# Two sets of PE transposes or one, for the flags of an expert selection inside an attention kernel

## The chip, the cores and the metric

The kernel runs on one core of a Trainium2 chip. A core has five engines that run their own instruction lists side by side and meet at semaphores: TensorE (PE; in the profile its weight loads have a row of their own, PEld), VectorE (DVE), ScalarE (ACT), GpSimd (POOL) and SyncE (SP, which here only issues transfers). The metric is the device time of one execution, in microseconds; less is better.

## The reference

Attention over 8 batches of 12 heads (448 positions, head size 64), causal, and behind it a mixture of experts with a limit on the tokens of an expert. The attention's output, 3584 rows of 768, is its input.

```python
def _moe_ref(x, w_gate, w1, w2, capacity):
    logits = x @ w_gate                              # 3584 x 8
    expert_idx = np.argmax(logits, axis=1)
    ...
    gate_w = probs[np.arange(N), expert_idx]
    for e in range(E):
        tok_idx = np.where(expert_idx == e)[0]
        if len(tok_idx) > capacity:                  # capacity is 80
            gw = gate_w[tok_idx]
            keep = np.argpartition(-gw, capacity)[:capacity]
            tok_idx = tok_idx[keep]
        h = np.maximum(x[tok_idx] @ w1[e], 0.0)
        out[tok_idx] = gate_w[tok_idx, None] * (h @ w2[e])
```

So each expert keeps the 80 tokens of the largest gate weight. What the change touches is how that choice is worked out while attention is still running.

## The kernel before

**Attention.** Two heads make a pair, six pairs a batch. The instruction order of every engine is written out by hand (`manual_schedule`): the loop over pairs runs over eight slots (k = 0 to 7) for each pair, and a slot issues one tile of the scores of this pair (`sp`, lines 423 to 436), in slots 0, 2, 4 and 6 a group of four transposes of the pair before (`tp`, line 465), in slot 7 the products with the values of the pair before that (`xp`, line 495). Behind each piece follows what reads it: DVE takes the scores with the mask and a maximum (`ns`, line 445; `nb` is its accumulator), ACT takes the exponential (`prob`, line 448) and copies the transposed tile out of PSUM (`PT`, line 477; for some pairs DVE does one of the four). The scores have three PSUM banks in turn, `tp` two. Every 16 slots a new third of the queries and keys is cast to fp16 and to the remainder: `L387` on DVE, `L384`, `L390`, `L391` and `L395` on POOL.

**The selection.** While the scores of batch b + 1 run, the selection of batch b is worked out in small steps, each with a due slot counted from the end of the batch: `STEPS` (lines 33, 34: `EARLY` takes its place for b = 6, the batch before the last). One slot can hold several steps; they are issued in the order of the dictionary, behind the slot's own work. For b = 7, the last batch, the steps run behind all the attention, in the order of `TAIL`.

The steps around the change, with their slots in STEPS:

- `weight`, `weighted` (28, 31): the gate weight of each token, and `ow`, the one-hot of its expert times that weight; POOL (DVE for some).
- `columns` (30, line 698): the flags. POOL writes the one-hot three times side by side into `oh3` (line 702), and one-hot times the number of the token in two pieces into `mv` (lines 703, 705).
- `parts` (33, lines 710 to 716): `ow` in three bf16 pieces, also into `mv`, four POOL instructions.
- `r0t`, `r0c` (32, 33): four PE transposes of `oh3` (128 x 128, line 731) into one PSUM bank `selt`, and DVE's copy of 24 rows of it into `ex[:, 0]` (line 734).
- `r1t`, `r1c` (34, 35): the same of the `ow` pieces in `mv`, into `ex[:, 1]`.
- `rl`, `lt`, `cp`, `ro` (36 to 41): the tokens against the table of the best 80 so far (`rl` reads `ex[:, 0]`), counted; `c3w` to `c0l` (38 to 46): the tokens of the batch against one another (`rn`, line 745, reads both halves of `ex`; `less`, line 748, is DVE's comparison).
- `gt`, `own`, `rank`, `places`, `rr`, `tn`, `tab`, `rp`, `row` (47 to 81): the new table. `tn` (77, line 862) reads `mv`; 81 is slot 33 of the next batch, so `rp` and `row` of batch b - 1 lie beside `r0t` and `r0c` of batch b.

All these PSUM tiles share the two banks "misc" of the pool `ps_m` in turn: each waits until the tile two before it has been read. `mv` and `oh3` have one buffer each, padded with zeros, since a transpose always reads 128 columns.

Of the kernel before, what the change touches and what calls it, by code (L numbers as in the profile page):

```python
# [10 lines left out]
BF16 = mybir.dt.bfloat16  # L11
# [6 lines left out]
P = 128  # L18
# [11 lines left out]
ROWGAP = 1  # L30
ROWS0 = [2, 3, 7, 13]
ROWS1 = [59, 62, 64, 65]
STEPS = {'gp': 18, 'gs': 18, 'lp': 21, 'lg': 22, 'logit': 23, 'shifted': 25, 'chosen': 26, 'sums': 27, 'one_hot': 28, 'weight': 28, 'weighted': 31, 'columns': 30, 'parts': 33, 'r0t': 32, 'r0c': 33, 'r1t': 34, 'r1c': 35, 'rl': 36, 'lt': 36, 'c3w': 38, 'c3l': 39, 'cp': 40, 'ro': 41, 'c2w': 41, 'c2l': 43, 'c1w': 43, 'c1l': 44, 'c0w': 46, 'c0l': 46, 'gt': 47, 'earlier': 51, 'own': 47, 'rank': 51, 'places': 63, 'places_more': 66, 'rr': 73, 'tn': 77, 'tab': 78, 'rp': 80, 'row': 81, 'rr_more': 75}
EARLY = {'gp': 18, 'gs': 18, 'lp': 21, 'lg': 21, 'logit': 22, 'shifted': 24, 'chosen': 26, 'sums': 27, 'one_hot': 28, 'weight': 29, 'weighted': 31, 'columns': 30, 'parts': 32, 'r0t': 33, 'r0c': 33, 'r1t': 34, 'r1c': 34, 'rl': 35, 'lt': 35, 'c3w': 36, 'c3l': 37, 'cp': 38, 'ro': 39, 'c2w': 39, 'c2l': 40, 'c1w': 40, 'c1l': 41, 'c0w': 41, 'c0l': 42, 'places': 43, 'places_more': 43, 'gt': 44, 'earlier': 44, 'own': 44, 'rank': 46, 'rr': 46, 'tn': 48, 'tab': 50, 'rp': 51, 'row': 52, 'rr_more': 46}
ROWS_EARLY = [22, 26, 29, 43]
THIRD = [0, 0, 2, 2, 4, 6, 8]
THIRD_NEXT = [0, 0, 6, 2, 6, 4, 8]
# [15 lines left out]
def attention_then_moe(  # L53
# [19 lines left out]
    NT = (S + P - 1) // P  # L73
# [24 lines left out]
    def bank(shape, dtype, name):  # L98
        return (ps_x or ps_m).tile(shape, dtype, name=name, tag="x" if ps_x else "misc")
# [20 lines left out]
    NV = 5  # L120
# [11 lines left out]
    for r in range(2):  # L132
        t = akeep.tile([P, OFF_L + NT * P], F32, name=f"prob{r}")
# [7 lines left out]
    for r in range(2):  # L141
        t = akeep.tile([P, NT, PH * P], F32, name=f"vt{r}")
# [79 lines left out]
    lg = keep.tile([P, NT, H * E], F32, name="lg")  # L222
# [28 lines left out]
    def late_constants():  # L251


        def padded(shape, name):
            t = spool.tile(shape, BF16, name=name, tag=name, bufs=1)
            nc.gpsimd.memset(t, 0.0)
            return t

        def orders():
            nonlocal identb, before  # L260
            identb = const.tile([P, P], BF16, name="identb")
            nc.gpsimd.tensor_copy(identb, ident)

            before = const.tile([P, NT * P], BF16, name="before")
            nc.gpsimd.memset(before, 1.0)
            own = before[:, (NT - 1) * P:NT * P]
            nc.gpsimd.affine_select(own, own, [[-1, P]], ALU.is_gt, 0.0, base=0, channel_multiplier=1)

        def gate_weights():
            nonlocal wgd  # L270

            wgd = const.tile([P, NP, 4 * E], F32, name="wgd")
            nc.gpsimd.memset(wgd, 0.0)
            for i in range(2):
                for j in range(2):
                    nc.gpsimd.tensor_copy(wgd[j * DH:(j + 1) * DH, i:NP:2, 2 * i + j:4 * E:4],
                                          wg_sb[j * DH:(j + 1) * DH, i:NP:2, :])

        def slots():
            nonlocal mv_flat, mv, slots_e, slots_t  # L280
            many = max(1, NSL)
            slots_e = const.tile([SL, many, E, SL], COUNT, name="slots_e")
            slots_t = const.tile([P, many, NT, SL], COUNT, name="slots_t")
            for t, k in ((slots_e, E), (slots_t, NT)):
                nc.gpsimd.iota(t, [[SL, many], [0, k], [1, SL]], base=0, channel_multiplier=0,
                               allow_small_or_imprecise_dtypes=True)
            mv_flat = padded([P, (NT - 1) * NV * E + 2 * E + P], "mv")
            mv = mv_flat[:, 0:NT * NV * E].rearrange("k (t v e) -> k t v e", v=NV, e=E)

        def operands():  # L290
            nonlocal oh_flat, one_hots, expert_cols, tables, table_rows
            oh_flat = padded([P, (NT - 1) * 3 * E + P], "oh3")
# [398 lines left out]
    def select_groups(bt):  # L691

        b = bt.b
        last = b == B - 1
# [2 lines left out]

        def columns():
            oh = bt.oh
            m, oh3 = bt.m, bt.oh3 = mv, one_hots  # L700
            bc = [P, NT, E]
            eng.tensor_copy(oh3, oh.unsqueeze(2).to_broadcast([P, NT, 3, E]))
            nc.gpsimd.tensor_tensor(out=m[:, :, 0, :], in0=oh, in1=tbase[:, b, :].unsqueeze(2).to_broadcast(bc),
                                    op=ALU.mult)
            nc.gpsimd.tensor_tensor(out=m[:, :, 1, :], in0=oh, in1=pnum.unsqueeze(2).to_broadcast(bc), op=ALU.mult)
            bt.parts = sm("parts", [P, NT])
            bt.less = [sm(f"less{t}", [P, (t + 1) * P], BF16) for t in range(NT)]
            bt.ex = expert_cols
# [14 lines left out]
        def expert_rows(i):  # L723
            got = []

            def turn():
                selt = bank([P, NT * P], BF16, "selt")
                got.append(selt)
                for t in range(NT):
                    src = mv_flat[:, (t * NV + 2) * E:][:, 0:P] if i else oh_flat[:, t * 3 * E:][:, 0:P]  # L730
                    nc.tensor.transpose(selt[:, t * P:(t + 1) * P], src, identb)

            def copy():
                (nc.scalar.copy if last else nc.vector.tensor_copy)(bt.ex[0:3 * E, i], got[0][0:3 * E])
            return [turn, copy]


        def compare(t):
            w = (t + 1) * P
            got = []  # L740

            def weights():
                rn = bank([P, NT * P], F32, "rn")
                got.append(rn)
                nc.tensor.matmul(rn[:, 0:w], bt.ex[:, 0, t * P:w], bt.ex[:, 1, 0:w], start=True, stop=True)

            def less():
                nc.vector.scalar_tensor_tensor(
                    out=bt.less[t], in0=got[0][:, 0:w], scalar=bt.gw[:, t:t + 1],
                    in1=before[:, NT * P - w:NT * P], op0=ALU.is_lt, op1=ALU.mult, accum_out=bt.parts[:, t:t + 1])  # L750
            return [weights, less]
# [90 lines left out]
        def move(s):  # L842
# [43 lines left out]
            if not last and NSL == 1:  # L886
# [3 lines left out]

        run = lambda fs: lambda: [f() for f in fs]
        bt.lower, bt.moves = [], []
        r0, r1 = expert_rows(0), expert_rows(1)
        cmp = [compare(t) for t in reversed(range(NT))]
        tabs = [table_chunk(s) for s in range(NSL)] if b else []
        moves = [f for s in range(NSL) for f in move(s)]
        steps = {"columns": columns, "parts": parts, "r0t": r0[0], "r0c": r0[1], "r1t": r1[0], "r1c": r1[1],
                 "places": places, "places_more": places_more, "earlier": earlier, "own": own, "rank": rank}
        steps.update({"hold": hold, **{f"gt{t}": lambda t=t: later_part(t) for t in range(NT)}} if last else {"gt": later})
        for t in range(NT):  # L900
# [38 lines left out]
    for b in range(B):  # L939
        bt = Batch()  # L940
# [17 lines left out]
    def batch_plan(bt):  # L958
# [23 lines left out]
    with tc.manual_schedule():  # L982
# [126 lines left out]
        for i, x in enumerate(ROW_ENGINES):  # L1109
            g, t = divmod(i, NT)  # L1110
# [331 lines left out]
```

## Time and profile before

| what | us |
|---|---|
| time, median of 3 runs (lowest to highest) | 466.85 (466.36 to 467.3) |
| the profiled execution's own time | 466.07 |
| its span, first to last instruction | 464.2 |
| transposes of `oh3`, 8 batches of 4 | x32, 217 to 230 ns each |
| transposes of `mv`, 8 batches of 4 | x32, 216 to 219 ns each |
| DVE's copies of `selt`, b = 0 to 6 | x14, 401 to 409 ns each |

The page gives each engine's busy time as a share of the span, and the chain that ended last: followed back from the last instruction, at each step to what released it. A row of the timeline is start, duration, engine, line, operation, output and inputs, count; in brackets, how long the engine was idle before it and who ended that. A matmul's duration has its latency in it; the distance to the next start shows how long it holds PE. In the windows view a row is the stretch, its length, the engine's busy time in it with the number of instructions, PE's granted clock, and the share and the rate of the DMA engines.

### The profile page before, as it was taken

What the parts mean: (1) busy time and instruction counts of PE and PEld (TensorE: products, weight loads), DVE (VectorE), ACT (ScalarE), POOL (GpSimd) and SP (SyncE); (2) the same over time, 40 slices, a digit from 0 to 9 for tenths busy, and PEclk for the clock granted to TensorE, in tenths of its full rate; (3) what the DMA queues carried; (4) which work ended last, traced back from release to release, by engine and by line L of the source; (5) the groups of instructions that cost most, each with busy time, mean ns of one, the idle gap of its engine ahead of it and who ended that gap; (6) DMA issues with size and microseconds to landing.
All of it is one profiled execution on the core that took longest, in us unless ns stands there. A gap on an engine that the chain in (4) does not pass through costs nothing.

```text
span 464.2 us, 14187 instructions
## 1 busy us (share of the span) xinstructions
PE 441.8 (95%) x4981; PEld 346.8 (75%) x4981; DVE 413.1 (89%) x1285; ACT 392.4 (85%) x1077; POOL 310.3 (67%) x382
## 2 busy tenths in 40 slices
PE   4899999999999999999999999999989999999994
PEld 2566667866777786677777767777648999999994
DVE  6888899988998999899899989989579999999892
ACT  6898989878988997898889789888586989988792
POOL 7999999988987987898798789860145133410011
PEclk9999999999999999999999999999999999999999
DMA  7758899989769578966957997539937999999941
GB/s 221 185 153 238 249 262 299 280 248 306 202 207 305 161 232 259 265 182 213 297 165 225 264 260 200 178 129 373 413 130 254 399 390 395 394 422 423 424 163 44
DMA packets 42998, 120.84 MB, mean 260 GB/s; under 512 B 6146, under 2 KB 23810, under 8 KB 39472
## 3 DMA queue, kind: packets, MB, share of 16 engines
q1 hardware_dynamic: 41712, 116.21, 76.9%
q0 software_dynamic: 1056, 3.51, 2.4%
q8 instruction: 39, 0.64, 0.6%
q14 instruction: 31, 0.25, 0.2%
q10 hardware_dynamic: 160, 0.23, 0.2%
HBM read 96.36 MB, written 23.99 MB: 259 GB/s over the span
## 4 chain that ended last, share of the span: by engine, by line
PE 83%; DVE 6%; DMA 3%; ACT 3%; issue 2%; SPq 1%; POOLq 0%; DVEq 0%
PE xp L495 16%; PE tp L465 15%; PE sp L423 6%; PE sp L424 5%; PE rt L592 4%; PE op L1245 4%; PE op L1237 4%; PE hp L1237 3%; PE gp L545 3%; PE hp L1252 3%; PE hp L1251 3%; PE hp L1249 3%; PE sp L433 3%; DMA qk<-k_t 3%; DVE ns L445 2%
## 5 line engine op out<-in xcount | busy, mean ns | idle before, releaser
L448 ACT ACTIVATE prob<-ns,nb 128x128 f32<-128x128 f32 (+3 forms) x336 | 177.0, 529 | 22.6 <-DVE nb L445 20.1
L445 DVE CUSTOM_DVE_ANT_0 ns<-sp,mask 128x384 f32<-128x384 f32 (+2 forms) x288 | 116.0, 413 | 18.7 <-PE sp L424 14.7
L465 PE MATMUL tp<-ident,prob 128*128 128x128 f32 x768 | 118.1, 276 | 0.9 <-ACT prob L448 0.9
L477 ACT COPY PT<-tp 128x512 f32<-128x512 f32 x182 | 104.0, 572 | 17.5 <-PE sp L423 8.4
L395 POOL TENSOR_TENSOR qk<-qk,qk 128x448 f16<-128x448 f32 x92 | 97.3, 1080 | 13.1 <-DVE qk L387 7.4
L465 PEld LDWEIGHTS tp<-ident,prob 128*128 128x128 f32 x768 | 89.6, 142 | 11.4 <-ACT prob L448 1.9
L1165 DVE SCALAR_TENSOR_TENSOR wl<-wraw,wh 128x768 f16<-128x768 f32 (+1 forms) x91 | 92.0, 1067 | 2.5 <-ACT wh L1180 2.3
L495 PE MATMUL xp<-PT,vt 128*64 128x448 f32 (+3 forms) x768 | 91.2, 380 | 0.0
L495 PEld LDWEIGHTS xp<-PT,vt 128*64 128x64 f32 x768 | 53.8, 137 | 42.7 <-issue 22.6
L423 PE MATMUL sp<-qk 128*128 128x384 f16 (+2 forms) x288 | 75.8, 279 | 8.0 <-DVE qk L349 5.1
L1180 ACT ACTIVATE wh<-wraw 128x768 f16<-128x768 f32 (+1 forms) x91 | 78.9, 931 | 4.2 <-PE hp L1252 1.8
L424 PE MATMUL sp<-qk 128*128 128x384 f16 (+2 forms) x288 | 78.1, 277 | 1.6 <-DVE qk L349 0.8
L448 ACT ACTIVATION_READ_ACCUMULATOR prob<-ns,nb 128x1 f32 x336 | 63.9, 190 | 0.0
L1338 POOL DMA_INDIRECT out<-yo,idx x8 | 14.6, 1828 | 69.0 <-ACT yo L1335 65.1
L390 POOL TENSOR_TENSOR qk<-qk,qk 64x448 f16<-64x448 f32 x46 | 54.2, 1179 | 3.4
L391 POOL TENSOR_TENSOR qk<-qk,qk 64x448 f16<-64x448 f32 x46 | 51.0, 1108 | 3.2
L387 DVE CAST qk<-qk 128x896 f16<-128x896 f32 x46 | 41.2, 897 | 1.1 <-DMA qk<-k_t 1.1
L423 PEld LDWEIGHTS <-qk 128*128 128x128 f16 x288 | 28.5, 99 | 17.1 <-issue 8.6
L384 POOL CAST qk<-qk 64x896 f16<-64x896 f32 x40 | 37.4, 936 | 4.3 <-PE sp L436 3.1
L1249 PEld LDWEIGHTS <-wh 128*128 128x128 f16 x362 | 36.5, 101 | 0.0
L1251 PEld LDWEIGHTS <-wh 128*128 128x128 f16 x362 | 36.2, 100 | 0.0
L1252 PEld LDWEIGHTS <-wl 128*128 128x128 f16 x362 | 36.2, 100 | 0.0
(192 smaller groups left out, 926.8 us busy)
## 6 DMA issues: line engine op xcount, KB each, us to landing
wraw<-w SPq DMA_DIRECT2D x27, 1536.0 KB, 20.4
qk<-k_t SPq DMA_DIRECT2D x92, 224.0 KB, 5.9
out<-mask_l SPq DMA_DIRECT2D x56, 192.0 KB, 4.4
qk<-q_t SPq DMA_DIRECT2D x23, 448.0 KB, 4.4
vt<-v_t SPq DMA_DIRECT2D x24, 384.0 KB, 5.9
xs<-xr SPq DMA_DIRECT2D x42, 192.0 KB, 3.9
wraw<-w SPq DMA_DIRECT2D x24, 256.0 KB, 6.1
vt<-v_t SPq DMA_DIRECT2D x24, 64.0 KB, 5.5
```

Of the source, the lines that this page charges most:

```text
L390: nc.gpsimd.tensor_tensor(out=qa[hi, i], in0=qf[lo, i], in1=qa[lo, i], op=ALU.subtract)
L391: nc.gpsimd.tensor_tensor(out=qb[lo, i], in0=qf[hi, i], in1=qb[hi, i], op=ALU.subtract)
L395: nc.gpsimd.tensor_tensor(out=k_lo[j][:, i], in0=kf[j][:, i], in1=k_hi[j][:, i], op=ALU.subtract)
L423: nc.tensor.matmul(sp[:, 0:w], qx[:, p, t * P:w], kx[:, p, 0:w], start=True, stop=False)
L424: nc.tensor.matmul(sp[:, 0:w], qx[:, p, t * P:w], lx[:, p, 0:w], start=False, stop=True)
L445: pr.masked = nc.vector.tensor_tensor_reduce(out=ns[:, 0:w], in0=sp[:, 0:w], in1=m, scale=-1.0 / 8.0, scalar=HUGE, op0=ALU.add, op1=ALU.mi ...
L448: nc.scalar.activation(pr.P[:, off:off + w], ns[:, 0:w], AF.Exp, bias=nb, scale=-1.0, accum_out=total)
L465: nc.tensor.transpose(pr.tp[:, i], pr.P[:, off:off + P], ident)
L477: copy(dst, src)
L495: state["pe"] = nc.tensor.matmul(xp[rows, 0:w], st["vt"][:, c, p * P + j * DH:p * P + (j + 1) * DH], pr.PT[:, j, n0:n0 + w], start=(c == 0 ...
L1165: return nc.vector.scalar_tensor_tensor(out=l, in0=src, scalar=SW, in1=h, op0=ALU.mult, op1=ALU.subtract)
L1180: nc.scalar.activation(h, src, AF.Copy, scale=SW)
```

## The change

In b = 0 to 6 one set of four transposes does for both kinds of flags. `mv` becomes 128 columns for each of the four token tiles (16 groups of 8 experts): the five pieces stand in groups 2 to 6, the three copies of the one-hot in groups 8 to 10 of the same block, and `columns` writes them there. A transpose of the whole block then holds the `ow` pieces in rows 32 to 55 and the one-hots in rows 64 to 87. The set is called `r1t` and stands where `r0t` was (slot 32; in `EARLY` slot 33, with `parts` left at 32); `parts` goes from slot 33 to 31. The two copies `r0c` and `r1c` keep their slots and read the same bank, the first from row 64, the second from row 32. The memset of `mv` grows from 264 to 544 columns. The last batch keeps `oh_flat` and its two sets.

```diff
-STEPS = {... 'columns': 30, 'parts': 33, 'r0t': 32, 'r0c': 33, 'r1t': 34, 'r1c': 35, 'rl': 36, 'lt': 36, ...}
-EARLY = {... 'parts': 32, 'r0t': 33, 'r0c': 33, 'r1t': 34, 'r1c': 34, 'rl': 35, 'lt': 35, ...}
+STEPS = {... 'columns': 30, 'parts': 31, 'r1t': 32, 'r0c': 33, 'rl': 36, 'lt': 36, 'r1c': 35, ...}
+EARLY = {... 'parts': 32, 'r1t': 33, 'r0c': 33, 'r1c': 34, 'rl': 35, 'lt': 35, ...}
...
-            mv_flat = padded([P, (NT - 1) * NV * E + 2 * E + P], "mv")
-            mv = mv_flat[:, 0:NT * NV * E].rearrange("k (t v e) -> k t v e", v=NV, e=E)
+            mv_flat = padded([P, NT * P + 4 * E], "mv")
+            mv = mv_flat[:, 0:NT * P].rearrange("k (t v e) -> k t v e", t=NT, e=E)
...
-            m, oh3 = bt.m, bt.oh3 = mv, one_hots
+            m = bt.m = mv[:, :, 2:2 + NV, :]
+            oh3 = bt.oh3 = one_hots if last else mv[:, :, 8:11, :]
...
-                    src = mv_flat[:, (t * NV + 2) * E:][:, 0:P] if i else oh_flat[:, t * 3 * E:][:, 0:P]
+                    src = mv_flat[:, t * P + 4 * E:][:, 0:P] if i else oh_flat[:, t * 3 * E:][:, 0:P]
...
-                (nc.scalar.copy if last else nc.vector.tensor_copy)(bt.ex[0:3 * E, i], got[0][0:3 * E])
+                nc.scalar.copy(bt.ex[0:3 * E, i], got[0][0:3 * E])
+
+        def both_rows():
+            got = []
+
+            def turn():
+                selt = bank([P, NT * P], BF16, "selt")
+                got.append(selt)
+                for t in range(NT):
+                    nc.tensor.transpose(selt[:, t * P:(t + 1) * P], mv_flat[:, t * P:(t + 1) * P], identb)
+
+            def copy(i):
+                r = 4 * E if i else 8 * E
+                nc.vector.tensor_copy(bt.ex[0:3 * E, i], got[0][r:r + 3 * E])
+            return [turn, lambda: copy(0), lambda: copy(1)]
...
-        r0, r1 = expert_rows(0), expert_rows(1)
+        rows = [f for i in range(2) for f in expert_rows(i)] if last else both_rows()
```

More of the change, by code (lines that the diff above doesn't have):

```diff
@@ L32 @@
 ROWS1 = [59, 62, 64, 65]
-STEPS = {'gp': 18, 'gs': 18, 'lp': 21, 'lg': 22, 'logit': 23, 'shifted': 25, 'chosen': 26, 'sums': 27, 'one_hot': 28, 'weight': 28, 'weighted': 31, 'columns': 30, 'parts': 33, 'r0t': 32, 'r0c': 33, 'r1t': 34, 'r1c': 35, 'rl': 36, 'lt': 36, 'c3w': 38, 'c3l': 39, 'cp': 40, 'ro': 41, 'c2w': 41, 'c2l': 43, 'c1w': 43, 'c1l': 44, 'c0w': 46, 'c0l': 46, 'gt': 47, 'earlier': 51, 'own': 47, 'rank': 51, 'places': 63, 'places_more': 66, 'rr': 73, 'tn': 77, 'tab': 78, 'rp': 80, 'row': 81, 'rr_more': 75}
-EARLY = {'gp': 18, 'gs': 18, 'lp': 21, 'lg': 21, 'logit': 22, 'shifted': 24, 'chosen': 26, 'sums': 27, 'one_hot': 28, 'weight': 29, 'weighted': 31, 'columns': 30, 'parts': 32, 'r0t': 33, 'r0c': 33, 'r1t': 34, 'r1c': 34, 'rl': 35, 'lt': 35, 'c3w': 36, 'c3l': 37, 'cp': 38, 'ro': 39, 'c2w': 39, 'c2l': 40, 'c1w': 40, 'c1l': 41, 'c0w': 41, 'c0l': 42, 'places': 43, 'places_more': 43, 'gt': 44, 'earlier': 44, 'own': 44, 'rank': 46, 'rr': 46, 'tn': 48, 'tab': 50, 'rp': 51, 'row': 52, 'rr_more': 46}
+STEPS = {'gp': 18, 'gs': 18, 'lp': 21, 'lg': 22, 'logit': 23, 'shifted': 25, 'chosen': 26, 'sums': 27, 'one_hot': 28, 'weight': 28, 'weighted': 31, 'columns': 30, 'parts': 31, 'r1t': 32, 'r0c': 33, 'rl': 36, 'lt': 36, 'r1c': 35, 'c3w': 38, 'c3l': 39, 'cp': 40, 'ro': 41, 'c2w': 41, 'c2l': 43, 'c1w': 43, 'c1l': 44, 'c0w': 46, 'c0l': 46, 'gt': 47, 'earlier': 51, 'own': 47, 'rank': 51, 'places': 63, 'places_more': 66, 'rr': 73, 'tn': 77, 'tab': 78, 'rp': 80, 'row': 81, 'rr_more': 75}
+EARLY = {'gp': 18, 'gs': 18, 'lp': 21, 'lg': 21, 'logit': 22, 'shifted': 24, 'chosen': 26, 'sums': 27, 'one_hot': 28, 'weight': 29, 'weighted': 31, 'columns': 30, 'parts': 32, 'r1t': 33, 'r0c': 33, 'r1c': 34, 'rl': 35, 'lt': 35, 'c3w': 36, 'c3l': 37, 'cp': 38, 'ro': 39, 'c2w': 39, 'c2l': 40, 'c1w': 40, 'c1l': 41, 'c0w': 41, 'c0l': 42, 'places': 43, 'places_more': 43, 'gt': 44, 'earlier': 44, 'own': 44, 'rank': 46, 'rr': 46, 'tn': 48, 'tab': 50, 'rp': 51, 'row': 52, 'rr_more': 46}
 ROWS_EARLY = [22, 26, 29, 43]
@@ L896, in select_groups @@
         moves = [f for s in range(NSL) for f in move(s)]
-        steps = {"columns": columns, "parts": parts, "r0t": r0[0], "r0c": r0[1], "r1t": r1[0], "r1c": r1[1],
+        steps = {"columns": columns, "parts": parts, **dict(zip(("r0t", "r0c", "r1t", "r1c") if last else ("r1t", "r0c", "r1c"), rows)),
                  "places": places, "places_more": places_more, "earlier": earlier, "own": own, "rank": rank}
```

## The prediction, made before the changed kernel ran

> **What bounds the kernel now.** I read the page first, engines and then the chain that ended last.
>
> ```profile
> PE 441.8 (95%) x4981; PEld 346.8 (75%) x4981; DVE 413.1 (89%) x1285; ACT 392.4 (85%) x1077; POOL 310.3 (67%) x382
> PE 83%; DVE 6%; DMA 3%; ACT 3%; issue 2%; SPq 1%; POOLq 0%; DVEq 0%
> ```
>
> TensorE (PE) is busy for 95% of the span and holds 83% of the chain, so taking work from PE looks like money in hand. But VectorE (DVE) has 89% and ScalarE (ACT) 85%: three engines run nearly abreast, and what PE gains in one place can be taken back at its next wait. So the question is which wait ends last behind each edit, and I read the timeline of each batch's selection steps, engine by engine. A slot is one eighth of a pair's stage; slot numbers are those of STEPS.
>
> **The steady batches (b = 1 to 5).** Here is b = 1, from the timeline of all engines; below it one row of the same timeline for b = 2, which shows the period, 150.44 - 110.00 = 40.44 us, and one of the chain, which shows that a group of four tp holds PE for 0.44 us.
>
> ```profile
> 109.16 0.25 POOL L716 TENSOR_TENSOR mv<-grest,mv 128x32 bf16<-128x32 f32 x1
> ...
> 110.00 0.39 PE L731 MATMUL selt<-identb,oh 128*128 128x128 bf16 x4
> ...
> 110.55 0.60 PE L465 MATMUL tp<-ident,prob 128*128 128x128 f32 x4
> ...
> 110.86 0.18 DVE L881 COPY row<-rp 24x80 bf16<-24x80 bf16 x1
> ...
> 111.16 0.24 PEld L731 LDWEIGHTS <-mv 128*128 128x128 bf16 x4 [0.24 <-issue]
> 111.19 0.38 PE L731 MATMUL selt<-identb,mv 128*128 128x128 bf16 x4
> ...
> 111.41 0.27 PE L423 MATMUL sp<-qk 128*128 128x256 f16 x1
> ...
> 112.17 0.07 DVE L445 DVE_READ_ACCUMULATOR2_ANT nb<- 128x1 f32 x1
> ...
> 112.53 0.33 PE L423 MATMUL sp<-qk 128*128 128x384 f16 x1
> ```
>
> ```profile
> 150.44 0.39 PE L731 MATMUL selt<-identb,oh 128*128 128x128 bf16 x4
> ```
>
> ```profile
> 109.67 0.44 PE tp L465 x4
> ```
>
> What goes is the set at 111.19. Its four transposes hold PE for 111.41 - 111.19 = 0.22 us (the 0.38 is mostly latency). Ahead of them is a hole: the tp before them began at 110.55, so PE was free at 110.55 + 0.44 = 110.99, and the set began at 111.19. It waited for its PSUM bank: the two "misc" banks go round, this set takes the one that rp had, and the row copy that empties it ends at 110.86 + 0.18 = 111.04. Removed are 0.22 of work and 0.20 of wait: **0.42 us per batch** at this spot. rl, the next user of a misc bank, then takes the bank of rp, free since 111.04; nothing new is late there.
>
> What is added: the remaining set, at 110.00, must now wait for the last of parts (L716) as well, not only for the flags. That ends at 109.41, 0.59 before; covered. If POOL were later than that, each batch would pay the difference. Moving parts from slot 33 to 31 changes no order: no other POOL step lies in slots 31 to 33 ahead of it, and L713 to L716 already follow the weighted step back to back.
>
> Does the 0.42 arrive? The same pair and the next, all engines, then PEld, then DVE's busy time in one stretch (length, busy, instructions):
>
> ```profile
> 109.82 0.29 DVE L445 CUSTOM_DVE_ANT_0 ns<-sp,mask 128x128 f32<-128x128 f32 x1 [1.18 <-PE sp L424]
> ...
> 114.75 0.54 DVE L445 CUSTOM_DVE_ANT_0 ns<-sp,mask 128x384 f32<-128x384 f32 x1
> ...
> 115.33 0.61 ACT L448 ACTIVATE prob<-ns,nb 128x384 f32<-128x384 f32 x1 [0.66 <-DVE nb L445]
> ...
> 117.40 0.21 DVE L779 TENSOR_SCALAR ro<-cp,pnum 80x8 f16<-80x8 f32 x1
> ...
> 117.69 0.27 PE L745 MATMUL rn<-ex 128*128 128x256 bf16 x1
> ...
> 118.33 0.57 ACT L477 COPY PT<-tp 128x512 f32<-128x512 f32 x1
> ```
>
> ```profile
> 118.94 0.42 PEld L465 LDWEIGHTS tp<-ident,prob 128*128 128x128 f32 x4 [0.29 <-ACT PT L477]
> ```
>
> ```profile
> 110.64:117.61 6.97, 6.97 (x35) 1.00 0.93 255
> ```
>
> DVE starts at 109.82, when PE delivers the pair's first scores, and is busy for all 6.97 us from 110.64 to 117.61, 35 instructions on end. None of them waits for the removed set but the second copy (r1c), which comes in its turn. At 114.75 it makes the scores that ACT has been idle for (0.66 us); ACT then runs without a break from 115.33 to the copy that ends at 118.33 + 0.57 = 118.90; and PE's tp of slot 46 stands waiting for exactly that bank, at 118.94. So PE's place at 118.94 is set by a path that leaves PE **before** the removed set, over DVE and ACT. On the way there is a second gate: the rn at 117.69 takes the bank that ro empties at 117.61, so at most some 0.03 survives even that far. I cost the five batches at **0.00**: the cover is DVE's list, and if it were 0.4 shorter, the 0.42 would show. The Trainium skill, Perfetto Trace Analysis, section "Identifying the Most-Contended Engine", says to take the engine of highest occupancy and optimize it first, though it warns that PE's matmul busy share is a poor measure. By occupancy that is PE and the whole 0.42 would count in each batch; the row at 118.94, where PE waits for ACT, speaks against it.
>
> **The first batch (b = 0).** Here POOL is behind. POOL's own timeline and its busy time from the memset of mv to the end of parts, then DVE's timeline, then PE's:
>
> ```profile
> 35.81 0.31 POOL L256 MEMSET mv<- 128x264 bf16 x1
> ...
> 43.10 0.95 POOL L256 MEMSET ex<- 128x1024 bf16 x1
> ...
> 68.95 0.27 POOL L702 CAST oh<-goh 128x96 bf16<-128x96 f32 x1
> ...
> 70.40 0.25 POOL L716 TENSOR_TENSOR mv<-grest,mv 128x32 bf16<-128x32 f32 x1
> 70.59 2.20 POOL L384 CAST qk<-qk 64x896 f16<-64x896 f32 x2
> ```
>
> ```profile
> 35.81:70.65 34.84, 33.24 (x44) 1.00 0.92 258
> ```
>
> ```profile
> 70.41 0.29 DVE L445 CUSTOM_DVE_ANT_0 ns<-sp,mask 128x128 f32<-128x128 f32 x1 [0.32 <-PE sp L424]
> ...
> 70.96 1.04 DVE L387 CAST qk<-qk 128x896 f16<-128x896 f32 x1
> ...
> 72.95 0.61 DVE L387 CAST qk<-qk 128x896 f16<-128x896 f32 x1
> ...
> 76.13 0.29 DVE L445 CUSTOM_DVE_ANT_0 ns<-sp,mask 128x128 f32<-128x128 f32 x1 [0.41 <-PE sp L424]
> ```
>
> ```profile
> 69.77 0.39 PE L731 MATMUL selt<-identb,oh 128*128 128x128 bf16 x4
> ...
> 72.40 0.32 PE L423 MATMUL sp<-qk 128*128 128x384 f16 x1 [0.27 <-DVE nb L445]
> ```
>
> The flags were cast in time for the set at 69.77; parts end at 70.65. The one set now needs both: it can start about 0.1 after that, at 70.75 (semaphore and weight load), so **0.98 us later** than 69.77. Queued behind it on PE are the next scores, and DVE, already idle for them at 70.41, waits 0.98 more. All that DVE does next moves along, the scores at 72.40 wait for DVE already, and at 76.13 DVE waits for PE again: PE and DVE are tied in turns, and I see no slack behind that returns the time. The removed set (0.22) pays nothing, since PE waits 0.27 at 72.40 anyway.
>
> The larger mv makes this worse. Its memset grows from 264 to 544 columns. From the rows 264 (0.310) and 1024 (0.947) a column costs 0.00084 us: +0.23, between 0 and the 0.64 to the 1024 row. POOL is busy 33.24 of the 34.84 us from there to L716, and what is left, 1.60 over 44 instructions, is 0.04 from one to the next and no wait, so this lag is carried to L716: **1.21 us** together. The DVE cast of 70.96 took 1.04 where its sister took 0.61: it ran beside POOL's casts. Shifted by 1.21 to 72.17 it falls into the second of them (the two took 2.20, now from 70.82), so I leave its length; without a collision it gives 0.43 back. The Trainium skill, SBUF — State Buffer, section "Who interferes with whom", says that such a DVE cast and a POOL instruction exclude each other for a whole instruction, whoever comes first; the 1.04 beside 0.61 agrees, and by it the cast waits for the second POOL cast as it did for the first.
>
> **The batch of EARLY (b = 6).** The set is in slot 33, parts stay at 32.
>
> ```profile
> 313.55 0.60 PE L465 MATMUL tp<-ident,prob 128*128 128x128 f32 x4
> ...
> 313.89 0.40 DVE L734 COPY ex<-selt 24x512 bf16<-24x512 bf16 x1
> ...
> 314.33 0.27 PE L423 MATMUL sp<-qk 128*128 128x256 f16 x1
> 314.44 0.28 PEld L761 LDWEIGHTS <-ex 128*128 128x128 bf16 x4
> ...
> 319.47 0.29 DVE L445 CUSTOM_DVE_ANT_0 ns<-sp,mask 128x128 f32<-128x128 f32 x1 [0.97 <-PE sp L424]
> ```
>
> The scores move from 314.33 to 313.99, but rl two slots on needs the first copy, which ends at 314.29; its weight load cannot begin before 314.33 instead of 314.44. **-0.11** remains, and since DVE waits for PE at 319.47, it is kept.
>
> Other edits. The two copies read PSUM rows 64 and 32 instead of 0, same shape; no row shows such a start: 0 each, at most the 0.17 by which ACT's copy of that shape is longer, which in DVE's full list would count 14 times (2.4 us). POOL writes with a wider stride: 0, hidden by the 0.59 in b = 1 to 5. The last batch keeps its two sets and its engines: 0.
>
> ```profile
> L734 DVE COPY ex<-selt x14: 401/406/409, 70.6 to 314.6; 24x512 bf16<-24x512 bf16 x14
> L734 ACT COPY ex<-selt x2: 575/575/575, 339.0 to 340.2; 24x512 bf16<-24x512 bf16 x2
> ```
>
> **The sum** against the profiled execution (466.07, of which the span is 464.2): +1.21 (b = 0), 0 (b = 1 to 5), -0.11 (b = 6), and -0.1 that I allow for the delay of b = 0 to shrink at later waits = **+1.0**: 467.1. That execution lies 0.78 under the median of the runs, 466.85; I add the +1.0 to the median: **467.8 us**. A measurement of this kernel can tell about 0.2% (0.93 us) from no change, so this lies at that bound.
>
> **Rivals.**
> 1. *Gains pass through* (ends on the other side). PE sets the end in each batch: -5 x 0.42 - 0.34 (314.33 to 313.99) + 1.21 = -1.2, 465.6. It decides as soon as DVE's list between 110.64 and 117.6 has 0.4 us of hidden waiting for PE. For it: PE's 95%. Against it: the waits at 117.69 and 118.94. Chance 0.10.
> 2. *Half pass.* PE runs ahead until the scores at slot 37 (112.53), whose bank DVE frees at 112.17 + 0.07; with 0.05 for the signal they could start at 112.29, and that 0.24 survives in each batch: -1.2 + 1.21 - 0.1 = 466.75. Chance 0.10.
> 3. *A cheaper stall in b = 0*: the memset's lag is lost on the way, or the cast of 70.96 meets no POOL cast: 0.98 - 0.43 - 0.11 = +0.4, 467.3. Chance 0.17.
> 4. *More than the stall*: copies from other rows longer, or POOL late in the steady batches too, 0.2 in each: +1.0 + 1.0 = 468.9. Chance 0.08.
> 5. Forecast, 467.3 to 468.4: chance 0.55, a little over half of it above 467.78.
>
> Range: 466.2 to 468.7 leaves out rival 1 and most of 4. Faster by over 0.2%: 0.10. Slower by over 0.2%: 0.31 + 0.08 + 0.02 = 0.41. Within: 0.49.
>
> **What would show it.** b = 0: the set starts near 71.0, PE shows a wait for POOL's L716 of about a microsecond, and everything to 104 lies 0.8 to 1.3 later. b = 1 to 5: set at the same place in the batch, no hole at 111, a new or longer wait of PE at slots 37, 43 and 46, and a period still of 40.44 us. If the period falls to about 40.0, rival 1 is right and my reading of DVE's list is wrong; if the set of b = 1 to 5 shows a wait for POOL, the 0.59 was no cover. b = 6: rl waits for the first copy.

## The result, and the profile after

| kernel | us, median (lowest to highest) | ratio to before, 95% interval |
|---|---|---|
| before, same chip | 466.61 (466.01 to 467.3), 4 runs | |
| changed | 473.26 (473.08 to 473.55), 4 runs | 1.0133 (1.0108 to 1.0157) |

The change costs 6.65 us, where +1.0 was forecast and the range ended at 468.7. First the engines and the chain that ended last, from the page of the changed kernel:

```profile
PE 441.1 (94%) x4953; PEld 344.1 (73%) x4953; DVE 417.8 (89%) x1285; ACT 392.8 (83%) x1077; POOL 309.6 (66%) x382
PE 73%; DVE 9%; DMA 8%; issue 4%; POOL 3%; ACT 2%; SPq 0%; POOLq 0%; DVEq 0%; ACTq 0%
```

PE has 28 matmuls less and 0.7 us less to do, as meant. But its share of the chain falls from 83% to 73%, DVE's rises from 6% to 9%, POOL enters with 3%, and DMA goes from 3% to 8%: PE waits more. For whom, these shares do not say: all but one of the transfers in this chain lie before 72 us, and a kernel tried below that is no slower than before (e5) has 5% of POOL and 4% of DMA in its chain. The starts of the one set, in PE's timeline of b = 0, 1 and 2 (lines from 702 on have moved: the set is now L745, DVE's copies L749, the last of parts L717, less L763):

```profile
70.76 0.40 PE L745 MATMUL selt<-identb,mv 128*128 128x128 bf16 x4 [0.74 <-POOL mv L717]
...
111.06 0.39 PE L745 MATMUL selt<-identb,mv 128*128 128x128 bf16 x4
...
152.62 0.39 PE L745 MATMUL selt<-identb,mv 128*128 128x128 bf16 x4
```

The first batch is as forecast: 70.76 stands 0.99 behind the 69.77 of before, and PE waits for POOL. The steady batches are not: 152.62 - 111.06 = 41.56 instead of 40.44, **1.12 us lost in every batch** where 0.00 was forecast. 0.99 + 5 x 1.12 = 6.6 of the 7.1 by which the spans differ (471.3 against 464.2). Executions reach this part of the kernel up to 1.1 apart (the memset of `mv` begins between 35.81 and 36.92), but in these two at the same time (35.81 and 35.82), so that the 0.99 can be read off as it stands.

Where in the batch? Here is DVE's timeline of b = 1 after the change; ns(0) began at 110.88:

```profile
111.92 0.18 DVE L896 COPY row<-rp 24x80 bf16<-24x80 bf16 x1
112.11 0.42 DVE L749 COPY ex<-selt 24x512 bf16<-24x512 bf16 x1
112.46 0.60 DVE L387 CAST qk<-qk 128x896 f16<-128x896 f32 x1
113.10 0.42 DVE L445 CUSTOM_DVE_ANT_0 ns<-sp,mask 128x256 f32<-128x256 f32 x1
...
113.79 0.08 DVE L445 DVE_READ_ACCUMULATOR2_ANT nb<- 128x1 f32 x1
113.90 0.42 DVE L749 COPY ex<-selt 24x512 bf16<-24x512 bf16 x1
114.25 0.60 DVE L387 CAST qk<-qk 128x896 f16<-128x896 f32 x1
114.89 0.56 DVE L445 CUSTOM_DVE_ANT_0 ns<-sp,mask 128x384 f32<-128x384 f32 x1
...
117.28 0.74 DVE L763 SCALAR_TENSOR_TENSOR less<-rn,ggw,before 128x512 bf16<-128x512 f32 x1
```

And the same rows of the kernel before, in its timeline of b = 1, as far as the prediction did not show them:

```profile
110.97 0.40 DVE L734 COPY ex<-selt 24x512 bf16<-24x512 bf16 x1
...
111.30 0.60 DVE L387 CAST qk<-qk 128x896 f16<-128x896 f32 x1
...
111.83 0.41 DVE L445 CUSTOM_DVE_ANT_0 ns<-sp,mask 128x256 f32<-128x256 f32 x1
...
112.52 0.07 DVE L445 DVE_READ_ACCUMULATOR2_ANT nb<- 128x1 f32 x1
112.52 0.41 DVE L734 COPY ex<-selt 24x512 bf16<-24x512 bf16 x1
...
115.77 0.73 DVE L748 SCALAR_TENSOR_TENSOR less<-rn,ggw,before 128x512 bf16<-128x512 f32 x1
```

The durations hardly differ (0.42 beside 0.40, 0.60 and 0.60). The starts do. In the full list of before, an instruction mostly begins a little ahead of the end of the one in front of it; where it begins only behind that end, I call it a hole. The first copy came 0.11 after row (110.86 to 110.97), now 0.19. The ns behind the cast came 0.53 after the cast's start, before its 0.60 had run out; now it comes 0.64 after, once the cast has ended. The second copy shows the same: 0.11 behind the start of the accumulator read, where before both began at 112.52, and 0.64 from cast to ns. From ns(0) to less DVE's full list takes 117.28 - 110.88 = 6.40 instead of 115.77 - 109.82 = 5.95. That is **0.45** per batch. The other 0.67 come 8 us later, at the cast of slot 49. Before, then after, from the timelines of DVE and POOL, and one group of PE's scores behind it:

```profile
123.57 0.62 DVE L387 CAST qk<-qk 128x896 f16<-128x896 f32 x1
123.60 1.49 POOL L390 TENSOR_TENSOR qk<-qk,qk 64x448 f16<-64x448 f32 x1
...
125.04 0.33 PE L423 MATMUL sp<-qk 128*128 128x384 f16 x1
```

```profile
124.99 1.03 POOL L390 TENSOR_TENSOR qk<-qk,qk 64x448 f16<-64x448 f32 x1
125.08 1.43 DVE L387 CAST qk<-qk 128x896 f16<-128x896 f32 x1
...
126.91 0.32 PE L423 MATMUL sp<-qk 128*128 128x384 f16 x1 [0.19 <-DVE nb L445]
```

Whichever begins first runs at its own length, and the other becomes longer: it ends 0.90 (POOL's, before) or 0.49 (DVE's, after) behind the end of the first. Before, DVE's cast was first by 0.03 us, and POOL paid (1.49 instead of 1.03). After, POOL is first by 0.09, and DVE pays, 1.43 instead of 0.62. POOL can afford it, DVE cannot: what it reads next is read later, and PE's scores wait for DVE (0.19 at 126.91, nothing at 125.04). The same order shows in all five steady batches: DVE leads by 0.03 to 0.04 before, POOL by 0.08 to 0.10 after.

### The profile page after: what moved, and what is told of

Same layout as the page of the kernel before. It is cut to its first block, busy times and chain, and to the rows that moved or that the text cites. A ratio compares the mean times of both kernels' runs of the same rounds, so it can differ in the third digit from the quotient of the medians.

```text
span 471.3 us, 14125 instructions
## 1 busy us (share of the span) xinstructions
PE 441.1 (94%) x4953; PEld 344.1 (73%) x4953; DVE 417.8 (89%) x1285; ACT 392.8 (83%) x1077; POOL 309.6 (66%) x382
## 4 chain that ended last, share of the span: by engine, by line
PE 73%; DVE 9%; DMA 8%; issue 4%; POOL 3%; ACT 2%; SPq 0%; POOLq 0%; DVEq 0%; ACTq 0%
PE xp L495 14%; PE tp L465 12%; PE sp L423 5%; PE sp L424 4%; PE op L1260 4%; DMA qk<-k_t 4%; PE op L1252 3%; DVE ns L445 3%; PE hp L1252 3%; PE rt L592 3%; PE hp L1266 3%; PE hp L1264 3%; PE hp L1267 3%; PE sp L433 3%; PE gp L545 3%
## 5 line engine op out<-in xcount | busy, mean ns | idle before, releaser
L395 POOL TENSOR_TENSOR qk<-qk,qk 128x448 f16<-128x448 f32 x92 | 96.0, 1063 | 16.3 <-DVE qk L387 10.6
L465 PEld LDWEIGHTS tp<-ident,prob 128*128 128x128 f32 x768 | 88.6, 141 | 14.2 <-ACT prob L448 4.9
L391 POOL TENSOR_TENSOR qk<-qk,qk 64x448 f16<-64x448 f32 x46 | 54.2, 1179 | 3.2
L390 POOL TENSOR_TENSOR qk<-qk,qk 64x448 f16<-64x448 f32 x46 | 52.2, 1135 | 3.4
L387 DVE CAST qk<-qk 128x896 f16<-128x896 f32 x46 | 44.2, 962 | 0.9 <-DMA qk<-k_t 0.9
L423 PEld LDWEIGHTS <-qk 128*128 128x128 f16 x288 | 28.2, 98 | 16.9 <-issue 8.2
L424 PEld LDWEIGHTS <-qk 128*128 128x128 f16 x288 | 28.4, 99 | 15.4 <-issue 12.7
```

What stands on the lines that cost most here:

```text
L390: nc.gpsimd.tensor_tensor(out=qa[hi, i], in0=qf[lo, i], in1=qa[lo, i], op=ALU.subtract)
L391: nc.gpsimd.tensor_tensor(out=qb[lo, i], in0=qf[hi, i], in1=qb[hi, i], op=ALU.subtract)
L395: nc.gpsimd.tensor_tensor(out=k_lo[j][:, i], in0=kf[j][:, i], in1=k_hi[j][:, i], op=ALU.subtract)
L423: nc.tensor.matmul(sp[:, 0:w], qx[:, p, t * P:w], kx[:, p, 0:w], start=True, stop=False)
L424: nc.tensor.matmul(sp[:, 0:w], qx[:, p, t * P:w], lx[:, p, 0:w], start=False, stop=True)
L465: nc.tensor.transpose(pr.tp[:, i], pr.P[:, off:off + P], ident)
```

## The experiments

Theory 1: copies that start at rows 64 and 32 cost DVE 0.22 each, and the delay turns an order between DVE and POOL. Theory 2, the rival: the shift is free, and the loss comes from the one set itself, its bank or its wait. All ratios are to runs of the kernel before on the same chip. The period is a quarter of the time from the set of b = 1 to that of b = 5 in PE's timeline; the list is from ns(0) to less in b = 1, and the cast's length is that of b = 1 too. Period, list and cast are of one profiled execution each.

| run | us, median | ratio, 95% interval | period | list | cast of slot 49 |
|---|---|---|---|---|---|
| before | | | 40.44 | 5.95 | 0.62 |
| changed | 473.26 | 1.0133 (1.0108 to 1.0157) | 41.56 | 6.40 | 1.43 |
| e1, shift alone | 473.81 | 1.0130 (1.0112 to 1.0148) | 41.59 | 6.41 | 1.43 |
| e2, second copy shifted | 472.13 | 1.0095 (1.0076 to 1.0114) | 41.34 | 6.17 | 1.43 |
| e3, first copy shifted | 468.49 | 1.0027 (0.9996 to 1.0058) | 40.65 | 6.16 | 0.62 |
| e4, POOL delayed | 471.02 | 1.0077 (1.0058 to 1.0097) | 40.91 | 6.40 | 0.62 |
| e5, DVE memset | 467.52 | 1.0005 (0.9990 to 1.0021) | 40.45 | 5.95 | 0.62 |
| e5b, DVE delayed | 470.70 | 1.0094 (1.0072 to 1.0117) | 41.22 | 5.95 | 1.47 |
| e6, two sets in b = 0 | 472.32 | 1.0120 (1.0103 to 1.0137) | 41.54 | 6.40 | 1.40 |
| e8, rows 64 to 64 | 480.40 | 1.0285 (1.0258 to 1.0312) | 42.73 | 7.94 | 1.05 |
| e10, two sets, ACT | 471.81 | 1.0118 (1.0092 to 1.0144) | 41.20 | 5.77 | 1.05 |
| e11, one set, ACT | 470.26 | 1.0071 (1.0056 to 1.0087) | 41.04 | 5.78 | 1.25 |
| e12, copies side by side | 473.82 | 1.0147 (1.0127 to 1.0166) | 41.49 | 6.70 | 1.05 |
| e14, set put back | 469.14 | 1.0042 (1.0027 to 1.0057) | 40.67 | 6.18 | 0.62 |

### The shift alone (e1)

```diff
-                    src = mv_flat[:, (t * NV + 2) * E:][:, 0:P] if i else oh_flat[:, t * 3 * E:][:, 0:P]
+                    src = mv_flat[:, (t * NV + 4) * E - r:][:, 0:P] if i else oh_flat[:, (t * 3 + 8) * E - r:][:, 0:P]
...
-                (...)(bt.ex[0:3 * E, i], got[0][0:3 * E])
+                (...)(bt.ex[0:3 * E, i], got[0][r:r + 3 * E])
```

> The kernel before, with its two sets of transposes, but each set's window begins 64 (one-hots) or 32 (ow pieces) columns earlier in padded tiles, so that the two copies of b = 0 to 6 read PSUM rows 64 and 32 and write row 0 as in the changed kernel. The shift (theory 1): DVE leaves about 0.1 ahead of each such copy and 0.1 behind the cast that follows, 0.45 per batch from ns(0) to less (6.40 instead of 5.95); and the cast of slot 49 then meets POOL's L390 and takes 1.43 instead of 0.62. Period 41.3 to 41.6 instead of 40.44, time 466.6 + 5 x 1.1 + about 0.5 for b = 0 and 6 = 472.5 (471 to 473.5); 469.3 if the cast does not meet POOL. One set, one bank, one wait (theory 2): the shift is free, 466.6 within 0.5.

With two sets, two banks and no new wait, only the start rows changed (and the padded tiles, which grow by 16 and 64 columns for it), and nearly the whole loss is there: ratio 1.0130 beside 1.0133, period 41.59 beside 41.56, list 6.41 beside 6.40, the same turned order. The stall of b = 0 is not in it; that 0.2% is within the two intervals. The time is 1.3 above the expected 472.5 and 0.3 above the upper end of the range. Theory 2 falls for the steady batches.

### One copy shifted, then the other (e2, e3)

```diff
-            m = bt.m = mv[:, :, 2:2 + NV, :]
-            oh3 = bt.oh3 = one_hots if last else mv[:, :, 8:11, :]
+            m = bt.m = mv[:, :, 4:4 + NV, :]
+            oh3 = bt.oh3 = one_hots if last else mv[:, :, 0:3, :]
...
-                r = 4 * E if i else 8 * E
+                r = 4 * E if i else 0
```

Above e2, where the order of the five pieces changes as well, so that those of `ow` come first; e3 has the pieces in groups 0 to 4, the one-hots in 8 to 10, and `r = 0 if i else 8 * E`.

> The changed kernel with other groups: one-hots in groups 0 to 2, the pieces in groups 4 to 8 (ow first), so that the first copy reads row 0 and only the second is shifted (row 32). Theory 1: half the loss on DVE, ns(0) to less 6.17; then 466.6 + 1.06 (b = 0) + 5 x 0.22 = 468.8 if the cast of slot 49 again comes ahead of POOL's L390, and 468.8 + 5 x 0.66 = 472.1 if it does not. No hole ahead of the first copy, one ahead of the second. Theory 2: 473.3 as the changed kernel, since set, bank and wait are the same.

> The changed kernel with the other half shifted: one-hots in groups 8 to 10 (the first copy reads row 64), the pieces in groups 0 to 4 with ow first (the second copy reads row 0). In the run with only the second copy shifted POOL's second L391 ended a fixed 0.9 after DVE's second cast, so the hole behind that cast delays DVE against POOL and turns the order at slot 49. Theory 1: here DVE loses 0.22 per batch around the first copy, none behind the second cast, the cast of slot 49 again begins 0.03 ahead of POOL's L390 and takes 0.62: period 40.44 + 0.22 = 40.66, time 466.6 + 1.06 + 5 x 0.22 = 468.8 (468.2 to 469.6), 3 us under the run with the other half. If the loss is simply in proportion to the shifted copies, 472.1 as that run. Theory 2: 473.3.

Both leave about half of the 0.45 on DVE's list (6.17 and 6.16, so 0.22 and 0.21). Yet one costs 0.90 per batch and the other 0.21. The difference is the order at slot 49. DVE and POOL in e3:

```profile
125.35 0.62 DVE L387 CAST qk<-qk 128x896 f16<-128x896 f32 x1
125.38 1.49 POOL L390 TENSOR_TENSOR qk<-qk,qk 64x448 f16<-64x448 f32 x1
```

The lead of before is back (0.02 to 0.03 in the five batches). Here is why. POOL is busy from the end of parts to this place, and held twice on the way by DVE's casts of slots 33 and 35; its second L391 ends 0.91 after DVE's second cast in the kernel before (112.89 + 1.48 against 112.86 + 0.60), 0.90 after it in the changed one (114.04 + 1.71 against 114.25 + 0.60), 0.91 in e2. So what DVE loses up to that cast, POOL loses too, and only a hole *behind* it counts between them. A shifted second copy puts 0.11 there, more than the lead of 0.03; a shifted first copy puts none. That was predicted before e3 ran (468.8, measured 468.49).

### The order at slot 49 (e4, e5, e5b)

```diff
             def q_low(i):
+                if h > HB and h % HB == 1 and i == 0:
+                    nc.gpsimd.tensor_tensor(out=scr, in0=number, in1=number, op=ALU.add)
```

```diff
             def k_high(j):
+                if h > HB and h % HB == 1 and j == 0:
+                    nc.vector.tensor_tensor(out=scr, in0=number, in1=number, op=ALU.add)
```

The first is e4, in the changed kernel; the second e5b, in the kernel before (e5 had a memset of one column in its place). Nobody reads `scr`.

> The changed kernel with one added POOL instruction (a sum of two 128 x 4 tiles that nobody reads, 0.28 from start to start by its neighbours) ahead of L390 of slot 51. If +0.66 of the +1.12 per batch is the DVE cast of slot 49 that finds POOL's L390 begun 0.09 earlier (theory 1), L390 now begins 0.19 behind the cast, the cast takes 0.62 and the period falls from 41.56 to about 40.9: 473.3 - 5 x 0.66 = 470.0 (469.3 to 471). If the +0.66 has another cause, 473.3 or up to 1.4 more for the added POOL work.

> The kernel before with one added DVE memset of one column (about 0.07) right ahead of the cast of slot 49. The cast leads POOL's L390 by 0.03 there. Theory 1: the order turns, the cast takes about 1.4 instead of 0.62, and the period grows by 0.07 + 0.66: 466.6 + 5 x 0.73 = 470.2 (469 to 471.5). If the order in which the two begin decides nothing: 466.6 + 6 x 0.07 = 467.0.

> As the run with the DVE memset, which hid beside its neighbours and left the cast 0.04 ahead of POOL, but with a sum of two 128 x 4 tiles (0.2) on DVE ahead of the cast of slot 49 in the kernel before. Theory 1: POOL's L390 now begins about 0.15 ahead, the cast takes 1.3 to 1.45 instead of 0.62 and ends 1.5 behind L390's start, 0.9 later than before: period 41.1 to 41.3, time 466.6 + 5 x 0.75 = 470.4 (469.3 to 471.5). If the order decides nothing: 466.6 + 6 x 0.23 = 468.0 at most.

POOL and DVE in e4, where the shifts stay and POOL gets one instruction more to do:

```profile
125.44 0.62 DVE L388 CAST qk<-qk 128x896 f16<-128x896 f32 x1
125.49 1.46 POOL L393 TENSOR_TENSOR qk<-qk,qk 64x448 f16<-64x448 f32 x1
```

DVE and POOL in e5b, the kernel before with one small DVE instruction more:

```profile
123.54 0.16 DVE L389 TENSOR_TENSOR scr<-number 128x4 f32<-128x4 f32 x1
123.61 1.47 DVE L390 CAST qk<-qk 128x896 f16<-128x896 f32 x1
...
123.55 1.05 POOL L393 TENSOR_TENSOR qk<-qk,qk 64x448 f16<-64x448 f32 x1
```

More work for POOL makes the changed kernel 0.65 per batch faster (41.56 to 40.91), and the 0.47 that it still has over the period of before is the 0.45 of DVE's list. DVE's addition moves the cast from 0.03 ahead of POOL to 0.06 behind it and costs 0.78 per batch, a ratio of 1.0094, with no shift anywhere. Expected were 470.0 and 470.4; 471.02 is just above its range, 470.70 inside. The memset of e5 missed: it ran beside the cast and delayed nothing, the cast kept a lead of 0.04, and the time did not change. So it says nothing about the order, and e5b took its place.

### The first batch, and the removed set (e6, e14)

```diff
-            oh3 = bt.oh3 = one_hots if last else mv[:, :, 8:11, :]
+            oh3 = bt.oh3 = one_hots if apart else mv[:, :, 8:11, :]
...
-        rows = [f for i in range(2) for f in expert_rows(i)] if last else both_rows()
+        rows = [f for i in range(2) for f in expert_rows(i)] if apart else both_rows()
```

Above e6, with `apart` true for b = 0 and 7; b = 0 has its old slots and unshifted copies there too. Below e14, on the kernel of e3:

```diff
-STEPS = {... 'r1t': 32, 'r0c': 33, 'rl': 36, ...}
+STEPS = {... 'r1t': 32, 'r0c': 33, 'rx': 34, 'rl': 36, ...}
...
-            return [turn, lambda: copy(0), lambda: copy(1)]
+            return [turn, lambda: copy(0), lambda: copy(1), turn]
```

> The changed kernel, but b = 0 keeps its two sets, its oh3 tile, its slots and unshifted copies; b = 1 to 6 are as changed, with the larger memset of mv. If the +1.06 by which the set of b = 1 came later is the wait for parts in b = 0: the first set at 69.8 to 70.0, the set of b = 1 at 110.0 to 110.3, the period still 41.56, and 473.3 - 1.0 = 472.3. If it is the memset or the two shifted copies of b = 0: half of it or all stays, 472.8 to 473.3.

> The one-set kernel with only the first copy shifted (468.5), with four transposes put back in slot 34 (33 + 1 in EARLY) of b = 0 to 6 into a bank that nobody reads: the second set's work on PE, and its turn in the two misc banks, without its copy. If the removed set was worth nothing in b = 1 to 5, as the prediction's step has it: period 40.65 as without it, 468.5 (468.1 to 469.1). If PE's 0.42 showed: period 41.0 to 41.1, 470.6.

In e6 the set of b = 1 begins 0.90 earlier than in the changed kernel (110.16), and the period stays. The median is 0.94 lower, as expected, but in another session, and the intervals of the two ratios overlap (1.0120 and 1.0133). In e14 PE has the second set again, and its two misc banks their old turns. PE's timeline, b = 1 and the last steady batch, b = 5:

```profile
111.20 0.39 PE L745 MATMUL selt<-identb,mv 128*128 128x128 bf16 x4
...
273.86 0.39 PE L745 MATMUL selt<-identb,mv 128*128 128x128 bf16 x4
```

(273.86 - 111.20) / 4 = 40.67, beside 40.65 without the set: four transposes and their bank are worth 0.02 per batch here, although in b = 1 they keep PE from its next scores for 0.34 (from 112.20, where the tp ahead of them lets PE go, to 112.54). The median is 0.65 above that of e3, but in another session, and the two ratios' intervals overlap.

### What DVE pays for (e8, e12)

```diff
-                (...)(bt.ex[0:3 * E, i], got[0][0:3 * E])
+                (...)(bt.ex[8 * E:11 * E, i], got[0][8 * E:11 * E])
...
-                (...)(row[0:3 * E, 0:sn], got["rp"][0:3 * E, 0:sn])
+                (...)(row[8 * E:11 * E, 0:sn], got["rp"][8 * E:11 * E, 0:sn])
```

Above e8, on the kernel before; in e12, on the changed kernel, `'r1c'` stands in slot 33 behind `'r0c'`.

> The kernel before, two sets, with everything at rows 64 to 87: both windows begin 64 columns earlier, the copies read row 64 and write row 64 of ex, and the table's transpose and row copy use rows 64 to 87 too. If a DVE copy pays for input and output rows that differ (theory 1): no holes, copies at 0.40, period 40.44, 466.6 to 467.2 (a little for the larger memsets in b = 0). If it pays for any start other than row 0: holes of 0.1 as in the run that shifts alone, a third around the row copy, 472 to 474.

> The changed kernel with the second copy moved right behind the first (slot 33), both ahead of the cast. In the run with rows 64 to 64 the holes stood where DVE goes from row 0 to another start and back, though input and output rows agreed; if it is the change of start rows between neighbours that costs 0.11, two copies side by side leave and return once: ns(0) to less 5.95 + 0.22 (0.33 if the step from 64 to 32 counts too) instead of 6.40, and no hole behind the second cast, so the cast of slot 49 stays ahead of POOL: period 40.7, 466.6 + 1.06 + 5 x 0.25 = 468.9 (468.3 to 470). If each shifted copy pays its 0.22 by itself: 6.40, and 469.9 without, 473.3 with the order turned at slot 49.

Both missed. DVE's timeline in e8:

```profile
112.98 0.08 DVE L445 DVE_READ_ACCUMULATOR2_ANT nb<- 128x1 f32 x1
113.10 0.20 DVE L881 COPY row<-rp 24x80 bf16<-24x80 bf16 x1
113.22 0.41 DVE L734 COPY ex<-selt 24x512 bf16<-24x512 bf16 x1
113.66 1.31 DVE L387 CAST qk<-qk 128x896 f16<-128x896 f32 x1
115.00 0.42 DVE L445 CUSTOM_DVE_ANT_0 ns<-sp,mask 128x256 f32<-128x256 f32 x1
```

Input and output rows agree, and the holes are there all the same: theory 1 as I had worded it for this run, that input and output differ, is wrong. Ahead of row a hole, between row and copy none (0.12 apart, 0.11 before). But now a hole stands *ahead of* the cast, 113.66 = 113.22 + 0.41 + 0.03, where the changed kernel has it behind. The holes ahead of it put the cast 0.20 behind POOL's L390 (113.46), where it was 0.04 ahead before (111.30 and 111.34): it takes 1.31, and its sister, behind POOL's L395, 1.20. The two make 1.31 of the 1.99 by which the list grew, and the cast of slot 49 is late as well (1.05). In e12:

```profile
112.92 0.18 DVE L896 COPY row<-rp 24x80 bf16<-24x80 bf16 x1
113.11 0.87 DVE L749 COPY ex<-selt 24x512 bf16<-24x512 bf16 x2
113.91 1.00 DVE L387 CAST qk<-qk 128x896 f16<-128x896 f32 x1
114.94 0.43 DVE L445 CUSTOM_DVE_ANT_0 ns<-sp,mask 128x256 f32<-128x256 f32 x1
```

The second copy begins 0.87 - 0.42 = 0.45 after the first, so it waited for its end too; then none ahead of the cast, one behind it: three holes instead of four. With the second copy ahead of it the first cast comes later than POOL's L390 (113.39) and takes 1.00, so the list grew to 6.70.

One reading fits every hole that I looked at, in the changed kernel, e1, e2, e3, e8 and e12: where it waits for no other engine, DVE begins an instruction while the one before is still running out, *unless* its input in PSUM starts in another group of 32 rows than the last PSUM input did, or its output in SBUF in another than the last output there; then it begins up to 0.04 after that one's end. By this the cast, which reads and writes SBUF at row 0, does not wait behind a copy from PSUM row 64 to SBUF row 0, but ns, the next to read PSUM, does: the hole behind the cast. In e8 the copy wrote SBUF at row 64, so the cast waits as well. The Trainium skill, VectorE: DVE Perf Modes, section "Two Vector instructions with no wait between them", states that rule, as a model: an instruction is held until every earlier one has finished if the start quadrant (a group of 32 rows) of an input differs from that last read in the same memory, or that of the output from the one last written there. The traces here agree with it at each place that I looked at, and add the price: 0.11 us per held instruction, 0.64 - 0.53 (0.08 for the first copy, 0.19 - 0.11). Only copies at rows 0, 32 and 64 were run, so that it is the group of 32 rows, and not the row itself, is not shown by these runs.

### The copy on ACT (e10, e11)

```diff
-                (nc.scalar.copy if last else nc.vector.tensor_copy)(bt.ex[0:3 * E, i], got[0][0:3 * E])
+                (nc.scalar.copy if last or b and i else nc.vector.tensor_copy)(bt.ex[0:3 * E, i], got[0][0:3 * E])
```

> The kernel before, two sets, no shift, with the second copy (r1c) of b = 1 to 6 on ACT instead of DVE. DVE's full list of slots 33 to 39 loses 0.34; ACT gets 0.57, beside the 0.66 that it idles for DVE ahead of the prob of slot 38. If DVE's list is the cover that kept the removed set of PE from showing, the period falls by 0.1 to 0.34: 466.6 - 5 x 0.2 = 465.6 (464.9 to 466.3). If rn of slot 38 waits longer for the later copy (ACT is busy without a break until about 113.8, the copy then ends 0.7 to 1.2 after DVE's did), PE loses 0.3 to 0.6 per batch there: 468 to 469.5.

> One set in b = 1 to 6 without any shifted copy on DVE: one-hots in groups 0 to 2 (DVE's copy reads row 0), ow pieces at row 32 copied by ACT in slot 34, b = 0 with its two sets. No hole on DVE, no stall in b = 0, the cast of slot 49 ahead of POOL. Theory 1 with the cover gone: the 0.42 of PE shows in part, period 40.1 to 40.4, 466.6 - 5 x 0.2 = 465.6 (464.8 to 466.8) or better than the run with two sets and ACT by up to 5 x 0.4. If ACT's added 0.57 delays prob and PT by as much as DVE gains: 466.6 to 467.5. Theory 2 (one set costs by itself): 471 or more.

Above e10, on the kernel before. In e11 b = 1 to 6 have one set with the one-hots at row 0 for DVE and the pieces at row 32 for ACT's copy (slot 34), and b = 0 keeps its two sets. I hoped for a version that beats the kernel before; neither does, and both missed. PE's rn waits for the copy, in e10 and then in e11:

```profile
114.40 0.38 PE L745 MATMUL rn<-ex 128*128 128x512 bf16 x1 [0.43 <-ACT ex L734]
```

```profile
113.92 0.38 PE L762 MATMUL rn<-ex 128*128 128x512 bf16 x1 [0.32 <-ACT ex L751]
```

And without the copy the second cast comes earlier and meets POOL too (0.77), so the list is shorter by 0.17 or 0.18 only. What that gives is lost again: PE's wait is passed on, and DVE idles for PE's scores behind the list (0.51 and 0.22 in e10, 0.16 and 0.22 in e11), which it did not before. From the set to the cast of slot 49 it is 13.57 before, 14.05 in e10, 13.69 in e11; there POOL is ahead, and the cast takes 0.43 or 0.63 more than 0.62. That is 0.48 + 0.43 = 0.91 and 0.12 + 0.63 = 0.75, of which 0.76 and 0.60 arrive in the period. In e11 the loss is mostly the turned order, in e10 the late copy costs as much.

## Why the prediction was wrong

**The step that failed** is the one on the other edits: "The two copies read PSUM rows 64 and 32 instead of 0, same shape; no row shows such a start: 0 each, at most the 0.17 by which ACT's copy of that shape is longer". Each shifted copy costs 0.22 in DVE's full list, so 0.45 per batch, and e1 shows it by itself. The bound was no bound: I took it from a *duration*, and the cost is not in the copy's duration (418 ns beside 406) but in when it and the next reader of PSUM may begin. Nor was the bound used: its 2.4 us for 14 copies are in neither the sum nor the range, and with them the forecast would have been 467.8 + 2.4 = 470.2. The rule of the Trainium skill (VectorE: DVE Perf Modes) that is told above would have put the holes at their places before any run; the prediction did not draw on it.

**What no term held** is the other 0.67 per batch: that a delay of DVE by 0.11 turns an order decided by 0.03. The prediction cited the lock of DVE's casts and POOL for b = 0 and left the steady batches alone. The two rows (123.57 and 123.60) were in the trace of before. Rival 4 came nearest: it named the copies from other rows, but as longer copies, priced them at 0.2 per batch, and had a chance of 0.08. Of the periods named as signs, neither 40.44 nor 40.0 came, but 41.56.

**b = 1 to 5, the removed set: right.** Costed at 0.00 under the cover of DVE's list; e14 measures 0.02. The hole of PE at 111 went as read, the new wait for parts never showed there, and nothing of the 0.42 arrived.

**b = 0: right in size, wrong in a part.** The stall was forecast at 0.98 and the row shows PE waiting 0.74 for POOL, the set 0.99 later; with two sets in b = 0 (e6) the set of b = 1 comes 0.90 earlier again. The 0.23 of the larger memset hardly arrived: it took 0.54 instead of 0.31, but POOL's first flag step began at 69.03 instead of 68.95 and its last at 70.46 instead of 70.40. So +1.21 was +1.0: POOL made up most of that lag on the way, which the prediction had ruled out.

**b = 6: wrong sign.** Costed at -0.11. From its set to that of the last batch before took 338.53 - 313.11 = 25.42, after 345.47 - 319.77 = 25.70: +0.28, and 25.45 in e3, where one copy is shifted. The rl went nearly as read: it waits for the first copy (0.38 in PEld's timeline) and comes 1.36 behind the set instead of 1.44. The loss is further on, at cp. Before, then after, from PE's timeline:

```profile
316.43 0.28 PE L774 MATMUL cp<-oh,lt 128*80 128x8 bf16 x4
```

```profile
323.38 0.28 PE L789 MATMUL cp<-mv,lt 128*80 128x8 bf16 x4 [0.19 <-DVE lt L782]
```

Four holes make DVE's last lt 0.47 later behind the set, cp now waits for it, and comes 3.61 behind the set instead of 3.32.

Together, in the profiled executions: 0.99 (b = 0) + 0.07 (from there to b = 1) + 5 x 1.12 + 0.28 (b = 6) + 0.16 behind it = 7.1, the difference of the spans. Of the 5 x 1.12, 2.25 are holes in DVE's list and 3.35 the turned order.

## What to carry to other kernels

Reading a tile at another start row is not free on DVE because its shape and duration are the same: count one hole for the instruction that changes the start row in PSUM or in SBUF from one of 0, 32 and 64 to another, and one for the next that changes it back, and place such copies where DVE waits anyway. Where two engines exclude each other, look up by how much the right one is first: an order won by 0.03 us is a price waiting to be paid, here 0.67 us per batch, more than the work that the change removed, and the cure can be to give the other engine *more* to do. And when a cost has no row, its bound must come from every way in which it could be paid, starts as well as durations.

## What the runs showed of the hardware

The holes follow the memory that an instruction touches: after a copy from row 64 of PSUM to row 0 of SBUF, a cast from SBUF to SBUF begins at once (0.35 after the copy's start, 0.33 before) and the next PSUM reader behind it is held. In the collisions the length of DVE's cast follows from POOL's lead: 1.47 with a lead of 0.06 (e5b), 1.43 with 0.09 (changed kernel), 1.25 with 0.27 (e11), 1.05 with 0.47 (e10: 124.09 against 124.56). Lead and length add up to 1.51 to 1.54 in all five steady batches of every run where POOL was ahead there: the cast ends a fixed time after POOL's instruction began, so that the loss is largest where the order is lost by least. Where the cast came first by as little as 0.01 (e14, b = 1 and 5), it kept its 0.62. What is left open is how much of such a loss PE passes on: at slot 49 the 0.81 became 0.67 of period. At slot 55 the cast takes 1.38 in both kernels, and whether that costs anything was not tried.
